# Subtracting the second part of x on VectorE from PSUM, and a state update with 48 columns per head

## The chip, the cores and the metric

The kernel runs on one NeuronCore of a Trainium2 chip. The metric is the device time of one execution in microseconds (us). Engines are named as the profile names them: PE is TensorE's matmul, PEld its weight load, DVE VectorE, ACT ScalarE, POOL GpSimd, SP SyncE (which only issues transfers here).

## The reference, cut to what matters

A linear recurrence with a complex decay per channel runs over 768 tokens for 4 batches and 8 heads of width 48. Its output, 3072 tokens of 384 values, goes through a gated feed-forward layer.

```python
for t in range(S):                                   # S = 768
    S_re, S_im = ar * S_re - ai * S_im, ar * S_im + ai * S_re
    S_re = S_re + outer(k[t], v[t])                  # 48 x 48 per head
    y[t] = q[t] @ S_re
x = y.reshape(3072, 384)
out = ((x @ w_a) * (x @ w_b)) @ w_out                # 384 -> 1536 -> 384
```

## The kernel before, in words

**Units.** The work is cut into 12 units: two batch pairs, each with 6 chunks of 128 tokens. A unit is 2 batches x 128 tokens, so 256 rows of x. For each unit there are four stages.

1. `prep(u)`, nearly all on DVE with some ACT: normalises the decay, forms its running products over the chunk, and multiplies them into q and divides them out of k. It is a Python generator that is advanced a little at a time. `stack(u)` then copies the result by DMA into `stk`, where each head has its 96 rows (48 real, 48 imaginary).
2. `attn(u)`, on PE with short DVE and ACT steps: for each batch i of the two, `scores` (k against q for 4 heads, then a causal mask multiplied in by DVE at L367), `transposes` (k into token rows, copied by ACT at L379), `outputs` (masked scores times v, plus the carried state times q, into the PSUM tile `xp`; ACT copies it at L408 into `xh`, rounded to fp32r), `residual` and `state`.
3. `gemm1(f)`: 18 matmuls for each of 12 blocks f of 128 hidden columns, in fp32r, with x and the weights each split into a rounded part and a remainder: xh·wh, xl·wh, xh·wl. ACT copies one half of the result (L475), DVE multiplies the other half in (L476), ACT rounds it (L477), DVE subtracts to get the remainder (L478).
4. `gemm2(f)`: 6 matmuls into the output, issued three blocks later (LAG = 3).

**The two steps that the change touches.** `residual` forms `xl` = x − `xh`. A matmul with minus the identity as weights (L412) adds −`xh` onto the 384 columns of `xp` still in PSUM, and an ACT copy (L415) takes the remainder out as fp32r. `state` multiplies the transposed k of a head (`kt`, 128 tokens x 96 rows, the weights) by v (the moving operand, 128 tokens x some columns) into a PSUM tile `pm`; DVE then adds it to the carried state `u` (L430), or ACT copies it for the first chunk (L432). In v's packed layout each pair of heads has 128 columns: 0 to 47 are the even head's, 48 to 79 zeros, 80 to 127 the odd head's. The kernel before streams 96 columns per head, 0 to 95 for the even head and 32 to 127 for the odd one, of which `kv` then picks 48. Four heads make a call; each fp32 matmul shows in the profile as two weight loads and two matmul records. `residual` runs 24 times, twice in each unit; `state` runs 40 times, four times in every unit that isn't the last chunk.

**The order.** Unit w's 12 blocks run in a loop. Between `gemm1(f)` and `gemm2` and after it there are slots, from f = 6 on (f = 5 for the first), in which the pieces of `attn(w+1)` are issued two at a time, `residual(0)` after `scores(1,0)` and `residual(1)` after `state(1,0)`. In between, `prep` of a later unit is advanced on DVE by a fixed estimated amount per block. Instructions of attention and of the feed-forward layer are given a higher priority than prep's, so on DVE they stand between prep's instructions. Every engine works its own list strictly in the order in which it was written, so an instruction that waits holds up all behind it. `pm` has two buffers (scores, transposes and state share them), `xp` one, the gemm1 tile `ab` three. PSUM tiles `pm` come free for the next transposes only when DVE has multiplied the mask in.

Of the kernel before, what the change touches and what calls it, by code (L numbers as in the profile page):

```python
# [14 lines left out]
ALU = mybir.AluOpType  # L15
PSUM = bass.MemoryType.PSUM

B, H, S, D = 4, 8, 768, 48
# [24 lines left out]
KS = 2 * D  # L43
# [14 lines left out]
def view(ap, offset, dims):  # L58
    return bass.AP(tensor=ap.tensor, offset=ap.offset + offset, ap=[list(ap.ap[0])] + dims)
# [7 lines left out]
def tile_kernel(ctx: ExitStack, tc: tile.TileContext, a_d, qk_d, v_d, w_d, qn_d, kn_d, vn_d, an_d, out_d):  # L67
    nc = tc.nc
    vec, act, pe, sync = nc.vector, nc.scalar, nc.tensor, nc.sync
# [43 lines left out]
    nident = const.tile([128, 128], F32, name="nident")  # L113
# [4 lines left out]
    def r(ap):  # L118
        return ap.bitcast(F32R)
# [76 lines left out]
    def rescaled(c):  # L196
        return c % 2 == 1 and c + 1 < NCH
# [152 lines left out]
    def attn(u, xh, xl):  # L350

        c = u % NCH
        last = c + 1 == NCH
        ams, kts, xps = {}, {}, {}

        def cols(i):
            return slice(i * C, (i + 1) * C), slice(TOK + i * C, TOK + (i + 1) * C)

        def scores(i, hg):
            qs, ks = cols(i)  # L360
            sp = ps_m.tile([128, 4, 128], F32, name="pm")
            for h4 in range(4):
                h = hg * 4 + h4
                pe.matmul(out=sp[:, h4], lhsT=stk[:, h, ks], rhs=stk[:, h, qs], start=True, stop=True)  # L364
            am = kvp.tile([128, 512], F32, name="am", bufs=2).rearrange("p (h t) -> p h t", h=4)
            with tc.high_priority(offset=ATTN_FIRST):
                vec.tensor_tensor(out=am, in0=sp, in1=mask[:].unsqueeze(1).broadcast_to([128, 4, 128]),  # L367
                                  op=ALU.mult)
            ams[i, hg] = am

        def transposes(i, hg):
            qs, ks = cols(i)
            tp = ps_m.tile([128, 512], F32, name="pm")
            for h4 in range(4):
                pe.transpose(out=tp[:, h4 * KS:(h4 + 1) * KS], in_=stk[0:KS, hg * 4 + h4, ks],
                             identity=ident[0:KS, 0:KS])
            kt = kvp.tile([128, 4, KS], F32, name="kt", bufs=2)
            with tc.high_priority(offset=ATTN_FIRST):
                act.copy(out=kt.rearrange("p h k -> p (h k)"), in_=tp[:, 0:4 * KS])  # L379
            kts[i, hg] = kt  # L380

        def outputs(i, half):
            qs, ks = cols(i)
            v_t = v_tiles[u, i]
            if half == 0:
                xps[i] = ps_x.tile([128, NJ, C], F32, name="xp")
            xp = xps[i]
            work = []
            for qd in range(4):
                lst = []  # L390
                for ti, pieces in quads[qd]:
                    mm = []
                    for h, off in pieces:
                        mm.append((v_t[:, off:off + 32], ams[i, h // 4][:, h % 4, :]))
                        if c > 0:
                            mm.append((us[i][:, off:off + 32], stk[:, h, qs]))
                    for n, (l, rr) in enumerate(mm):
                        lst.append((ti, l, rr, not lst, n == len(mm) - 1))
                work.append(lst)
            ns = len(work[0])  # L400
            for n in range(half * ns // 2, (half + 1) * ns // 2):
                for qd in range(4):
                    ti, l, rr, st, sp_ = work[qd][n]
                    pe.matmul(out=xp[qd * 32:(qd + 1) * 32, ti], lhsT=l, rhs=rr, start=st, stop=sp_,  # L404
                              tile_position=(0, qd * 32), skip_group_check=True)
            if half == 1:
                with tc.high_priority(offset=ATTN_FIRST):
                    act.copy(out=r(xh[:, :, qs]), in_=xp)  # L408

        def residual(i, _):  # L410
            qs, ks = cols(i)
            pe.matmul(out=xps[i], lhsT=r(nident), rhs=r(xh[:, :, qs]), start=False, stop=True,  # L412
                      skip_group_check=True)
            with tc.high_priority(offset=ATTN_FIRST):
                act.copy(out=r(xl[:, :, qs]), in_=xps[i])  # L415

        def state(i, hg):
            ut, v_t = us[i], v_tiles[u, i]
            kp = ps_m.tile([128, 512], F32, name="pm")
            for h4 in range(4):  # L420
                h = hg * 4 + h4
                o = (h // 2) * 128 + (h % 2) * 32
                pe.matmul(out=kp[0:KS, h4 * 96:(h4 + 1) * 96], lhsT=kts[i, hg][:, h4, :],
                          rhs=v_t[:, o:o + 96], start=True, stop=True)
            uv = view(ut[0:KS], hg * 256, [[128, 2], [80, 2], [1, 48]])
            kv = view(kp[0:KS], 0, [[192, 2], [144, 2], [1, 48]])
            sv = view(stk[0:KS], hg * 4 * RUN + 2 * TOK + i, [[2 * RUN, 2], [RUN, 2], [0, 48]])
            with tc.high_priority(offset=ATTN_FIRST):
                if c > 0:
                    vec.tensor_tensor(out=uv, in0=kv, in1=uv, op=ALU.add)  # L430
                else:
                    act.copy(out=uv, in_=kv)  # L432
                if rescaled(c):
                    vec.tensor_tensor(out=uv, in0=uv, in1=sv, op=ALU.mult)

        order = [(scores, 0, 0), (scores, 0, 1), (transposes, 0, 0), (transposes, 0, 1),
                 (outputs, 0, 0), (outputs, 0, 1), (scores, 1, 0), (residual, 0, 0), (state, 0, 0), (scores, 1, 1),
                 (state, 0, 1), (transposes, 1, 0), (transposes, 1, 1), (outputs, 1, 0),
                 (outputs, 1, 1), (state, 1, 0), (residual, 1, 0), (state, 1, 1)]
        if u == 0:  # L440
            order = [(scores, 0, 0), (scores, 0, 1), (outputs, 0, 0), (outputs, 0, 1), (scores, 1, 0), (scores, 1, 1),
                     (residual, 0, 0), (outputs, 1, 0), (outputs, 1, 1), (transposes, 0, 0), (transposes, 0, 1),
                     (residual, 1, 0), (state, 0, 0), (state, 0, 1), (transposes, 1, 0), (transposes, 1, 1),
                     (state, 1, 0), (state, 1, 1)]
        for fn, i, g in order:
            if not (last and fn in (transposes, state)):
                fn(i, g)
                yield
# [292 lines left out]
```

## Time and profile before

| what | value |
|---|---|
| three timed runs | 701.16, 704.75, 705.05 us (median 704.75) |
| the profiled execution's own time | 703.08 us |
| its span from first to last instruction | 701.3 us (1.8 us lie around it) |
| mean granted clock of TensorE | 0.981 |
| PE / PEld / DVE / ACT busy | 654.5 / 608.7 / 553.0 / 319.0 us |
| `residual` matmul L412, ACT copy L415 | 24 of each |
| `state` matmul L423 | 320 records (40 calls x 4 heads x 2) |

Matmul records are pipelined: a gemm1 matmul lasts 0.28 us in the trace while the next one starts 0.11 to 0.12 us after it. So the distance between starts, not the duration, is what a matmul costs PE, and PE shows as busy even where it loses a little. On DVE, too, an instruction's record overlaps the next one's by some tens of nanoseconds.

### The profile page before, as it was taken

Reading aid. Unit: us, or ns where it says so; the run is one execution under the profiler, and the core shown is the slowest. Engines: PE = TensorE matmul, PEld = TensorE weight load, DVE = VectorE, ACT = ScalarE, POOL = GpSimd, SP = SyncE. Lnnn points to the kernel's source line nnn. Section 1 sums busy time; section 2 is a strip of 40 time slices with the busy share of each in tenths; the row PEclk is TensorE's granted clock in tenths of the full one; section 3 lists DMA queues with packets and bytes.
Section 4 is the critical chain, followed back from the end, with each engine's and each line's share of the span. In section 5 each row is a group of like instructions: output and inputs, shape, how many; then the busy total and the mean of one; then the engine's idle time right before and its main releaser. Section 6 shows DMA issues by size and latency. Waiting matters only on the chain.

```text
span 701.3 us, 14492 instructions
## 1 busy us (share of the span) xinstructions
PE 654.5 (93%) x5862; PEld 608.7 (87%) x5862; DVE 553.0 (79%) x1387; ACT 319.0 (45%) x642; POOL 5.6 (1%) x11
## 2 busy tenths in 40 slices
PE   3657899999999999999999999999999999999997
PEld 1224788899898999999999998999999999999996
DVE  6999899898988989989799898999989963232221
ACT  6347666634635446255453554635543332232221
POOL 3000000000000000000000000000000000000000
PEclk9985999999999999999999999999999999999999
DMA  8963300511404206034051250511510510400000
GB/s 317 402 254 91 121 0 2 181 55 46 136 31 141 80 16 197 23 100 122 29 145 59 89 145 2 166 68 47 131 59 2 134 55 7 115 23 2 22 2 28
DMA packets 30233, 63.95 MB, mean 91 GB/s; under 512 B 3664, under 2 KB 7248, under 8 KB 30160
## 3 DMA queue, kind: packets, MB, share of 16 engines
q1 hardware_dynamic: 26704, 58.23, 26.4%
q10 hardware_dynamic: 3456, 4.72, 1.9%
q8 instruction: 48, 0.79, 0.5%
q14 instruction: 25, 0.20, 0.1%
HBM read 39.32 MB, written 4.72 MB: 63 GB/s over the span
## 4 chain that ended last, share of the span: by engine, by line
DVE 55%; PE 31%; ACT 6%; DMA 5%; issue 2%; SPq 0%; DVEq 0%; ACTq 0%
PE ab L467 13%; PE o L485 8%; DVE pr L226 6%; DVE qk L294 5%; DVE a_t L274 5%; DVE z L232 4%; DVE h_t L476 4%; DVE hl L478 4%; PE xp L404 3%; DMA w<-in_dram 3%; PE pm L364 3%; DVE z L279 3%; DVE pb L253 2%; DVE am L367 2%; DVE b_t L259 2%
## 5 line engine op out<-in xcount | busy, mean ns | idle before, releaser
L467 PE MATMUL ab<-xh,w 128*128 128x256 f32 x1728 | 332.5, 282 | 0.0
L467 PEld LDWEIGHTS ab<-xh,w 128*128 128x128 f32 x1728 | 275.6, 189 | 1.9 <-issue 1.0
L467 PE MATMUL ab<-xl,w 128*128 128x256 f32 x864 | 242.2, 280 | 0.0
L467 PEld LDWEIGHTS ab<-xl,w 128*128 128x128 f32 x864 | 162.6, 188 | 0.0
L485 PE MATMUL o<-w,hh 128*128 128x384 f32 x576 | 151.8, 344 | 0.0
L476 DVE TENSOR_TENSOR h_t<-ab,h_t 128x256 f32<-128x256 f32 x144 | 60.3, 419 | 71.3 <-ACT h_t L475 71.3
L475 ACT COPY h_t<-ab 128x256 f32<-128x256 f32 x144 | 53.0, 368 | 133.4 <-PE ab L467 132.3
L477 ACT CAST hh<-h_t 128x256 fp32r<-128x256 f32 x144 | 58.1, 404 | 107.9 <-DVE h_t L476 107.5
L485 PEld LDWEIGHTS o<-w,hh 128*128 128x128 f32 x576 | 96.5, 188 | 3.5 <-issue 3.4
L485 PE MATMUL o<-w,hl 128*128 128x384 f32 x288 | 97.8, 340 | 0.0
L478 DVE TENSOR_TENSOR hl<-h_t,hh 128x256 fp32r<-128x256 f32 x144 | 60.4, 419 | 18.0 <-ACT hh L477 17.8
L226 DVE TENSOR_TENSOR pr<-z 128x192 f32<-128x192 f32 (+1 forms) x195 | 65.2, 341 | 6.0 <-ACT z L212 1.2
L364 PE MATMUL pm<-stk 128*128 128x128 f32 x384 | 55.7, 283 | 4.9 <-DMA stk<-qk 4.3
L364 PEld LDWEIGHTS pm<-stk 128*128 128x128 f32 x384 | 50.2, 195 | 9.0 <-issue 6.4
L146 PE MATMUL ab<-o_sb,ident 128*128 128x384 f32 x42 | 30.6, 830 | 27.3 <-DVE o_sb L137 27.3
L485 PEld LDWEIGHTS o<-w,hl 128*128 128x128 f32 x288 | 54.1, 188 | 0.6 <-issue 0.4
L232 DVE TENSOR_TENSOR z<-pr 128x96 f32<-128x96 f32 (+1 forms) x195 | 47.2, 248 | 3.7
L404 PE MATMUL xp<-am,v_t 128*32 128x128 f32 x768 | 42.2, 277 | 3.8 <-DVE am L367 3.6
L274 DVE TENSOR_TENSOR a_t<-z,b_t 128x768 f32<-128x768 f32 x48 | 45.3, 950 | 0.0
L146 PEld LDWEIGHTS ab<-o_sb,ident 128*128 128x128 f32 x42 | 10.7, 296 | 37.3 <-DVE o_sb L137 27.3
L294 DVE TENSOR_TENSOR qk<-qk,z 128x1536 f32<-128x1536 f32 (+1 forms) x26 | 42.3, 1627 | 0.2
L367 DVE TENSOR_TENSOR am<-pm,mask 128x512 f32<-128x512 f32 x48 | 32.8, 684 | 6.8 <-PE pm L364 6.7
(100 smaller groups left out, 756.5 us busy)
## 6 DMA issues: line engine op xcount, KB each, us to landing
w<-in_dram SPq DMA_DIRECT2D x36, 384.0 KB, 7.9
qk<-in_dram SPq DMA_DIRECT2D x12, 768.0 KB, 4.8
stk<-qk SPq DMA_DIRECT2D x48, 192.0 KB, 3.3
a_t<-in_dram SPq DMA_DIRECT2D x11, 768.0 KB, 4.4
v_t<-in_dram SPq DMA_DIRECT2D x24, 256.0 KB, 2.7
stk<-qk SPq DMA_DIRECT2D x24, 192.8 KB, 3.3
out_dram<-o_sb ACTq DMA_DIRECT2D x24, 192.0 KB, 2.0
stk<-qk SPq DMA_DIRECT2D x16, 128.0 KB, 3.1
```

What stands on the lines that cost most here:

```text
L226: vec.tensor_tensor(out=pr[:, :, :, o:o + n], in0=view(zz, W + at_(i) + 2 * o, [[W, 2], [-W, 2], [2, n]]), in1=tok(slice(1, 3), i - 1, o, ...
L232: vec.tensor_tensor(out=tok(slice(1, 3), i, o, n), in0=pr[:, :, 0, o:o + n], in1=pr[:, :, 1, o:o + n], op=ALU.add)
L274: vec.tensor_tensor(out=pz[:, s].rearrange("p (j b e) -> p j b e", j=SUB // 2, e=2), in0=zb[:, 1 + s], in1=view(bb, (1 + k - s) * NB, [[0, ...
L294: vec.tensor_tensor(out=qk4[:, :, k, x0:x1], in0=qk4[:, :, 1, x0:x1], in1=z[:, k].rearrange("p (j t) -> p j t", j=NJ).unsqueeze(2).broadca ...
L364: pe.matmul(out=sp[:, h4], lhsT=stk[:, h, ks], rhs=stk[:, h, qs], start=True, stop=True)
L404: pe.matmul(out=xp[qd * 32:(qd + 1) * 32, ti], lhsT=l, rhs=rr, start=st, stop=sp_, tile_position=(0, qd * 32), skip_group_check=True)
L467: pe.matmul(out=ab[:, m * TOK:(m + 1) * TOK], lhsT=r(w_ab(f, part, m * NJ + i)), rhs=r(xt[:, i, :]), start=n == 0, stop=n == 8)
L475: act.copy(out=h_t, in_=ab[:, 0:TOK])
L476: vec.tensor_tensor(out=h_t, in0=ab[:, TOK:2 * TOK], in1=h_t, op=ALU.mult)
L477: act.copy(out=r(hh), in_=h_t)
L478: vec.tensor_tensor(out=r(hl), in0=h_t, in1=hh, op=ALU.subtract)
L485: pe.matmul(out=os_[tt][:, 0:DM], lhsT=r(ht[:, ts]), rhs=r(w_t[f, 2][:, part, :]), start=(f == 0 and n == 0), stop=(f == NF - 1 and n == 2))
```

## The change

`residual` no longer uses PE or ACT: DVE subtracts `xh` from the PSUM tile `xp` and writes `xl`. `state` streams only the 48 columns that a head owns, so the four results lie side by side in 192 columns and the picking view `kv` changes with them. Nothing else is changed: the buffers, the slots and the priorities stay.

```diff
         def residual(i, _):
             qs, ks = cols(i)
-            pe.matmul(out=xps[i], lhsT=r(nident), rhs=r(xh[:, :, qs]), start=False, stop=True,
-                      skip_group_check=True)
             with tc.high_priority(offset=ATTN_FIRST):
-                act.copy(out=r(xl[:, :, qs]), in_=xps[i])
+                vec.tensor_tensor(out=r(xl[:, :, qs]), in0=xps[i], in1=xh[:, :, qs], op=ALU.subtract)
 
         def state(i, hg):
             ut, v_t = us[i], v_tiles[u, i]
             kp = ps_m.tile([128, 512], F32, name="pm")
             for h4 in range(4):
                 h = hg * 4 + h4
-                o = (h // 2) * 128 + (h % 2) * 32
-                pe.matmul(out=kp[0:KS, h4 * 96:(h4 + 1) * 96], lhsT=kts[i, hg][:, h4, :],
-                          rhs=v_t[:, o:o + 96], start=True, stop=True)
+                o = (h // 2) * 128 + (h % 2) * 80
+                pe.matmul(out=kp[0:KS, h4 * D:(h4 + 1) * D], lhsT=kts[i, hg][:, h4, :],
+                          rhs=v_t[:, o:o + D], start=True, stop=True)
             uv = view(ut[0:KS], hg * 256, [[128, 2], [80, 2], [1, 48]])
-            kv = view(kp[0:KS], 0, [[192, 2], [144, 2], [1, 48]])
+            kv = view(kp[0:KS], 0, [[2 * D, 2], [D, 2], [1, D]])
```

## The prediction, made before the changed kernel ran

> **What bounds the kernel now.** I read the shares first, then the chain that ended last, because shares alone would name PE.
>
> ```profile
> PE 654.5 (93%) x5862; PEld 608.7 (87%) x5862; DVE 553.0 (79%) x1387; ACT 319.0 (45%) x642; POOL 5.6 (1%) x11
> ```
> ```profile
> DVE 55%; PE 31%; ACT 6%; DMA 5%; issue 2%; SPq 0%; DVEq 0%; ACTq 0%
> ```
>
> PE is busy for 93% of the span, yet DVE holds 55% of the chain. DVE's 79% is an average over two stages, which the table by stretches separates (columns: length, PE, PEld, DVE, ACT busy).
>
> ```profile
> 428.00:473.00 45.00, 44.76 (x454) 43.45 (x455) 41.51 (x102) 22.49 (x44) 0.00 (x0) 1.00 0.30 92
> 558.00:605.00 47.00, 47.00 (x474) 45.85 (x473) 20.70 (x40) 16.22 (x36) 0.00 (x0) 1.00 0.19 57
> ```
>
> While prep runs, DVE is busy 41.5 of 45 us; when prep has ended, 20.7 of 47. What this costs PE is seen in the times at which three successive units start, by their first gemm1 matmul (PE's rows in order of time; units 8, 9 and 10, counted from 0):
>
> ```profile
> 506.42 0.28 PE L467 MATMUL ab<-xh,w 128*128 128x256 f32 x1
> ...
> 557.98 0.28 PE L467 MATMUL ab<-xh,w 128*128 128x256 f32 x1
> ...
> 608.30 0.28 PE L467 MATMUL ab<-xh,w 128*128 128x256 f32 x1
> ```
>
> Units 8 and 9 give PE the same work. Unit 8, with most of a prep beside it, takes 51.56 us, unit 9 50.32. So DVE costs about 1.2 us a unit, and the waits from 250 to 520 us say where:
>
> ```profile
> PEld pm L375 <- DVE am L367: 4.4, 7, 1.6
> ```
> ```profile
> DVE a_t L288 <- ACT a_t L282: 7.5, 7, 1.6
> DVE a_t L303 <- ACT a_t L290: 3.2, 4, 1.9
> ...
> DVE h_t L476 <- ACT h_t L475: 0.3, 1, 0.3
> ```
>
> Transposes wait for a `pm` buffer until DVE has masked the scores. DVE itself waits almost only for ACT's part of prep, and for the feed-forward layer 0.3 us in 270: it is behind PE. The chain shows the end of that state:
>
> ```profile
> 542.81 0.34 DVE hl L478
> 543.14 0.61 DVE am L367
> 543.75 0.05 issue
> 543.80 0.55 PE pm L375 x4
> ```
>
> Up to 543.75 us the chain is mostly DVE, from there on PE alone. So a microsecond added to DVE before 543 should arrive at the end, one taken from PE counts in full only behind it.
>
> **Part 1, the subtraction. What it takes from PE.**
>
> ```profile
> 553.10 0.18 PE xp L412
> ```
> ```profile
> L415 ACT CAST xl<-xp 128x384 fp32r<-128x384 f32 x24 | 11.5, 479 | 12.8 <-PE xp L412 12.6
> ```
>
> The first row is of the chain: an L412 holds PE for 0.18 us, its weight load lying beside the matmul ahead of it. So PE loses 24 x 0.18 = 4.3 us of work. On the PE part of the chain behind 543.75 us lie five of them: the one at 553.10 (second of `attn(9)`) and two each of `attn(10)` and `attn(11)`: **-0.9 us**. The others leave PE earlier at a `pm` wait that DVE ends: nothing, unless DVE is quicker than I think. ACT loses 24 x 0.479 = 11.5 us; at 45% busy, and with no L415 on the chain pieces that I followed, I count that as nothing. If ACT did hold the chain, its 6% share would bound the gain.
>
> **What it adds to DVE.** No 128x384 tensor_tensor stands in the trace, but its neighbours do:
>
> ```profile
> L478 DVE TENSOR_TENSOR hl<-h_t,hh 128x256 fp32r<-128x256 f32 x144 | 60.4, 419 | 18.0 <-ACT hh L477 17.8
> L476 DVE TENSOR_TENSOR h_t<-ab,h_t 128x256 f32<-128x256 f32 x144 | 60.3, 419 | 71.3 <-ACT h_t L475 71.3
> ...
> L137 DVE SCALAR_TENSOR_TENSOR o_sb<-w,o_sb 128x384 uint32<-128x384 uint32 x36 | 19.6, 550 | 0.1
> ```
>
> 384 elements take 550 ns. From PSUM (L476) and from SBUF (L478) 256 elements take the same 419 ns, so the PSUM operand adds nothing. [...]
>
> What the queue loses is the distance between starts. The chain's pieces above give 0.34 for 256 elements (542.81) and 0.61 for 512 (543.14), so about 0.47 for 384. Between two dependent prep instructions it is less, since part of it fills the gap between them:
>
> ```profile
> 416.42 0.36 DVE L226 TENSOR_TENSOR pr<-z 128x192 f32<-128x192 f32 x1
> 416.69 0.42 DVE L478 TENSOR_TENSOR hl<-h_t,hh 128x256 fp32r<-128x256 f32 x1
> 417.03 0.25 DVE L232 TENSOR_TENSOR z<-pr 128x96 f32<-128x96 f32 x1
> 417.31 0.36 DVE L226 TENSOR_TENSOR pr<-z 128x192 f32<-128x192 f32 x1
> 417.71 0.26 DVE L232 TENSOR_TENSOR z<-pr 128x96 f32<-128x96 f32 x1
> 418.00 0.36 DVE L226 TENSOR_TENSOR pr<-z 128x192 f32<-128x192 f32 x1
> ```
>
> A pr-z pair takes 0.89 us with an hl in it (416.42 to 417.31) and 0.69 without (to 418.00), so an instruction that costs 0.34 alone costs 0.20 there. For 384 elements that makes 0.33 to 0.47; I take 0.40, as both kinds of place occur. Fifteen subtractions lie before 543 us in the stage where DVE holds the chain (two each of `attn(2)` to `attn(8)`, one of `attn(9)`): **+6.0 us** (5.0 to 7.1). Those of `attn(0)` and `attn(1)` lie where weight conversion, DMA and PE hold much of the chain: between 0 and 4 x 0.47 = 1.9; I take **+0.7**. The rest fall where DVE is half idle: nothing. If one falls into a wait for ACT (10.7 us in the 270 above), it is free there.
>
> **The wait it adds.** The subtraction waits for ACT's `xh` (L408), and everything behind it on DVE with it: prep, h_t, hl, the masks.
>
> ```profile
> 536.04 0.48 ACT L408 CAST xh<-xp 128x384 fp32r<-128x384 f32 x1 [0.59 <-PE xp L404]
> ```
>
> Since DVE runs behind PE before 543, I take no wait; its bounds are nothing and a whole L408 copy, 0.48 us, each time. Readers of `xl` and the next writer of `xp` come several microseconds of PE work later.
>
> **Part 2, 48 columns.** Halving the moving columns helps only if streaming sets the pace of these matmuls. PE's rows around one call, and the load behind it:
>
> ```profile
> 502.60 0.84 PE L423 MATMUL pm<-v_t,kt 128*96 128x96 f32 x8
> 503.23 0.36 PE L467 MATMUL ab<-xh,w 128*128 128x256 f32 x1
> 503.43 0.28 PE L467 MATMUL ab<-xl,w 128*128 128x256 f32 x1
> ```
> ```profile
> 503.20 0.19 PEld L467 LDWEIGHTS ab<-xh,w 128*128 128x128 f32 x1
> ```
>
> Eight records run from 502.60 to where the last starts, about when the next load does (503.20): 0.60 / 7 = 85 ns each. [...] The first gemm1 matmul behind the call shows what a load then costs: it lasts 0.36 instead of 0.28 us, because its 128-column load began only at 503.20. Loads by columns:
>
> ```profile
> L423 PEld LDWEIGHTS pm<-v_t,kt 128*96 128x96 f32 x320 | 32.2, 164 | 2.1 <-issue 1.4 <-ACT hh L477 0.2 <-DVE z L232 0.2
> L404 PEld LDWEIGHTS xp<-am,v_t 128*32 128x32 f32 x768 | 24.0, 109 | 11.2 <-DVE am L367 5.7 <-issue 2.4 <-ACT xl L415 0.2
> ...
> L375 PEld LDWEIGHTS pm<-ident,stk 96*128 96x128 f32 x160 | 16.2, 143 | 6.5 <-DVE am L367 5.3 <-ACT kt L379 0.2 <-issue 0.2
> ```
>
> From 32 to 96 columns a load grows by 55 ns, 0.86 ns a column; 96 columns are 83 ns, the 85 of the pace. The weights, `kt`, keep their 96 columns. So I take **0** for part 2. Against it speaks that transposes load 128 columns in 143 ns, so not every load goes at that rate. The other bound is that streaming sets the 85 ns: then each record falls to about 43 and PE loses 320 x 42 ns = 13.4 us.
>
> [...]
>
> **The sum.** +6.0 + 0.7 - 0.9 = +5.8 us. The profiled execution took 703.1, so 708.9, and I forecast **709**. The median of the runs shown is 1.7 higher; the bounds and that give 705 to 714 for this case alone. About 1%, 7 us, is what can be told from no change here.
>
> **Rivals.**
>
> *DVE has room after all* (22%). For it: DVE is idle 3.5 of 45 us, and its list is written anew, so subtractions could fall into its waits for ACT. Then PE's 4.3 us are what is left: 698.8. Against it: with room on DVE the chain would not have run 55% there, nor would the masks come late in unit after unit.
>
> *Streaming sets the pace of state* (9%), and PE, so relieved, sets the end: 703.1 - 4.3 - 13.4 = 685.4. For it: a matmul that streams fewer columns keeps the array for less time. Against it: the late load above. If streaming set the pace and DVE still held the chain, only the 4 x 8 records of `attn(10)` in unit 9 would count, 32 x 42 ns = 1.3 us, which stays inside the forecast's range. [...]
>
> *DVE waits for `xh` at the head of its list* (12%). Twenty subtractions before 558 us wait 0.48 each: 9.6 more, 718.5. It decides once the mask and h_t work on DVE is less behind PE than the copy takes; DVE's rows show 0.3 us of waiting for gemm1, which speaks against it.
>
> *The edit does nothing to the work* is excluded for part 1; for part 2 it is my forecast, though PE's records must show 48 columns.
>
> The forecast itself has 52%, and 5% is left for a cause that I don't see. The range 696 to 715 takes the forecast's own and most of the first rival, and leaves out the second and the third. Against the median of 704.75, over 1% is below 697.7 or above 711.8: faster 18% (the second rival and some of the first), slower 30% (the third and the forecast's upper end), within 1% 52%.
>
> **What would show it.** 24 DVE subtractions of about 550 ns and no L412; state records still 85 ns apart, their matmuls shorter; DVE busy about 43 of 45 us in mid-kernel, with longer waits of L375 for the mask; units 9 and 10 0.35 us shorter. State records at 45 ns apart, or DVE waits named after ACT's `xh`, would prove me wrong.

## The result and the profile after

The median after is 708.65 us (707.15 to 710.16, six runs) against 704.64 before: ratio 1.0064, 95% interval [1.0047, 1.0082]. The kernel is 0.6% slower, about 4 us. The profiled execution after, 710.16, is the slowest of its six, that before, 703.08, lies 1.6 under its median, so the traces show 7.1 us between their spans (701.3 and 708.4). The forecast of 709 was right as a number. Its place was wrong: the loss is made in unit 0, and the middle of the kernel, where the sum put +6, did not become slower.

The page of the kernel after, engine shares and the chain by engine:

```profile
PE 658.3 (93%) x5838; PEld 608.8 (86%) x5838; DVE 565.0 (80%) x1411; ACT 309.6 (44%) x618; POOL 5.6 (1%) x11
...
PE 48%; DVE 37%; ACT 5%; DMA 5%; issue 2%; SPq 1%; DVEq 0%; ACTq 0%
```

DVE has 24 instructions and 12 us more, yet its share of the chain fell from 55% to 37%. That alone speaks against "DVE held the chain and now holds it more". The groups of the two edited lines (subtraction, state) and PE's rows around one state call, all of after; lines behind L413 carry numbers two lower than before:

```profile
L413 DVE TENSOR_TENSOR xl<-xp,xh 128x384 fp32r<-128x384 f32 x24 | 13.2, 550 | 3.8 <-ACT xh L408 3.8
L421 PE MATMUL pm<-v_t,kt 128*96 128x48 f32 x320 | 32.9, 246 | 0.1
```
```profile
457.89 0.80 PE L421 MATMUL pm<-v_t,kt 128*96 128x48 f32 x8
458.51 0.36 PE L465 MATMUL ab<-xh,w 128*128 128x256 f32 x1
```

The subtraction takes 550 ns from PSUM, as its SBUF neighbour did, and waited 3.8 us for `xh` in the whole kernel. A call of eight state records with 48 moving columns leaves PE to gemm1 after 458.51 − 457.89 = 0.62 us; with 96 columns it was 503.23 − 502.60 = 0.63.

Where the time went is seen from the start of the feed-forward of unit 0 and of unit 1 (PE's rows in order of time; before, then after):

```profile
80.86 0.36 PE L467 MATMUL ab<-xh,w 128*128 128x256 f32 x1
...
149.97 0.36 PE L467 MATMUL ab<-xh,w 128*128 128x256 f32 x1
```
```profile
79.88 0.60 PE L465 MATMUL ab<-xh,w 128*128 128x256 f32 x3
...
156.88 0.60 PE L465 MATMUL ab<-xh,w 128*128 128x256 f32 x3
```

Unit 0 takes 77.0 us instead of 69.1. From the start of unit 1 to the end it is 708.4 − 156.9 = 551.5 after and 701.3 − 150.0 = 551.3 before. So all of it is made before 157 us. Behind that point units 2 to 4 and 9 lose 3.1 us, units 5 to 8 gain 4.1, unit 11 loses 1.5.

In unit 0 the two chains differ at one place, the end of `prep(1)` (before, then after; start, length, what; L294 is prep's last multiply into q and k):

```profile
125.17 1.67 DVE qk L294
126.86 3.42 DMA stk<-qk
130.32 0.49 PE pm L364 x2
```
```profile
129.28 1.67 DVE qk L294
130.95 0.34 DVE h_t L474
131.29 0.51 DVE qk L294
131.79 1.07 issue
132.87 0.43 DVE hl L476
133.30 0.27 SPq L331
...
135.68 4.23 DMA stk<-qk
139.95 0.81 PE pm L364 x2
```

Before, prep's last multiply starts at 125.1 us and `stk` reaches the scores of `attn(1)` from 130.3 on. After, it starts at 131.2, the first piece of `stk` comes at 136.40 and the last at 139.95. What PE does meanwhile (after, PE's rows; in brackets the idle time ahead and what ended it):

```profile
134.14 0.34 PE L483 MATMUL o<-w,hl 128*128 128x384 f32 x1
136.40 1.01 PE L364 MATMUL pm<-stk 128*128 128x128 f32 x4 [1.92 <-DMA stk<-qk]
138.79 0.46 PE L364 MATMUL pm<-stk 128*128 128x128 f32 x2 [1.38 <-DMA stk<-qk]
139.95 1.49 PE L364 MATMUL pm<-stk 128*128 128x128 f32 x4 [0.70 <-DMA stk<-qk]
```

PE has used up all of unit 0's gemm2 by 134.5 and can do nothing but wait. Before, gemm2 matmuls still stood between the scores, the last of them at 139.1 us. A second thing happens here, in the table by stretches (length, PE, PEld, DVE, ACT, POOL busy, then the granted clock; before, then after):

```profile
140.00:144.00 4.00, 3.49 (x58) 3.11 (x47) 3.86 (x10) 2.15 (x4) 0.00 (x0) 1.00 0.33 117
```
```profile
136.00:140.00 4.00, 1.48 (x7) 0.94 (x7) 3.18 (x9) 2.84 (x4) 0.00 (x0) 0.93 0.88 268
140.00:144.00 4.00, 3.91 (x31) 2.75 (x32) 2.97 (x9) 2.43 (x4) 0.00 (x0) 0.50 0.49 133
144.00:148.00 4.00, 3.43 (x25) 2.96 (x28) 3.22 (x8) 1.88 (x3) 0.00 (x0) 0.71 0.63 201
```

Just when PE has work again its clock is halved, for 0.6 + 4.0 + 2.3 = 6.9 us by the three shares (a stretch at 0.71 is half-speed for 0.58 of it); stretches cut at its edges place it from 139.46 to 146.29 us, 6.8 us.

Over the whole kernel the waits turned around (60 to 710 us; total, times, longest; before, then after):

```profile
PE pm L364 <- DMA stk<-qk: 4.3, 4, 1.7
...
PE pm L375 <- DVE am L367: 3.4, 7, 1.3
```
```profile
PE pm L364 <- DMA stk<-qk: 9.3, 9, 1.9
...
PE pm L375 <- DVE am L367: 0.6, 2, 0.4
```

The transposes' wait for the mask, which I had expected to grow, nearly vanished; the wait for `stk` doubled, and 4.0 of its 9.3 us lie in unit 0 (0.7 of the 4.3 before).

### The profile page after: what moved, and what is told of

Its sections match the earlier page's. It is cut to its first block, busy times and chain, and to the rows that moved or that the text cites. A ratio compares the mean times of both kernels' runs of the same rounds, so it can differ in the third digit from the quotient of the medians.

```text
span 708.4 us, 14429 instructions
## 1 busy us (share of the span) xinstructions
PE 658.3 (93%) x5838; PEld 608.8 (86%) x5838; DVE 565.0 (80%) x1411; ACT 309.6 (44%) x618; POOL 5.6 (1%) x11
## 4 chain that ended last, share of the span: by engine, by line
PE 48%; DVE 37%; ACT 5%; DMA 5%; issue 2%; SPq 1%; DVEq 0%; ACTq 0%
PE ab L465 21%; PE o L483 10%; PE xp L404 6%; PE pm L364 4%; DVE qk L294 4%; DVE a_t L274 4%; DVE pr L226 4%; PE pm L421 3%; DMA stk<-qk 3%; DVE hl L476 3%; DVE h_t L474 3%; DVE z L232 2%; PE pm L375 2%; DVE z L279 2%; DVE pb L253 2%
## 5 line engine op out<-in xcount | busy, mean ns | idle before, releaser
L364 PE MATMUL pm<-stk 128*128 128x128 f32 x384 | 60.7, 291 | 10.1 <-DMA stk<-qk 9.3
L364 PEld LDWEIGHTS pm<-stk 128*128 128x128 f32 x384 | 52.3, 199 | 16.4 <-issue 9.9
L404 PE MATMUL xp<-am,v_t 128*32 128x128 f32 x768 | 45.2, 283 | 2.7 <-DVE am L367 2.7
L294 DVE TENSOR_TENSOR qk<-qk,z 128x1536 f32<-128x1536 f32 (+1 forms) x26 | 42.3, 1628 | 0.1
```

Of the source, the lines that this page charges most:

```text
L294: vec.tensor_tensor(out=qk4[:, :, k, x0:x1], in0=qk4[:, :, 1, x0:x1], in1=z[:, k].rearrange("p (j t) -> p j t", j=NJ).unsqueeze(2).broadca ...
```

## The experiments

Each ratio is to the kernel before, which ran again beside each group: its medians were 703.13 (e1 to e4), 702.93 (e5 to e8) and 703.16 (e9, e10), so a ratio is not the quotient of the medians in this table. "prep(1)" is when DVE starts prep(1)'s last L294, "unit 1" when its first gemm1 matmul starts, "between" the time from one to the other, "half clock" how long TensorE ran at half rate from 120 to 160 us, "rest" the span minus "unit 1". These five come from the one profiled execution of each. That execution lies within 1 us of its kernel's median but for before (1.6 below), e10 (1.7 below), e8 (1.3 above), after (1.5 above), e9 (2.0 above) and e4 (4.4 above).

| kernel | median us | ratio, interval | prep(1) | unit 1 | between | half clock | rest |
|---|---|---|---|---|---|---|---|
| before | 704.64 | | 125.1 | 150.0 | 24.9 | 0 | 551.3 |
| after | 708.65 | 1.0064 [1.0047, 1.0082] | 131.2 | 156.9 | 25.7 | 6.8 | 551.5 |
| e1 part 1 alone | 704.72 | 1.0020 [1.0006, 1.0033] | 127.5 | 151.0 | 23.4 | 0 | 551.8 |
| e2 part 2 alone | 702.77 | 0.9999 [0.9986, 1.0011] | 126.6 | 150.0 | 23.5 | 0 | 550.9 |
| e3 from unit 2 on | 702.10 | 0.9981 [0.9966, 0.9995] | 126.6 | 150.1 | 23.5 | 0 | 550.2 |
| e4 units 0, 1 only | 709.15 | 1.0073 [1.0054, 1.0092] | 131.3 | 158.5 | 27.2 | 10.2 | 553.3 |
| e5 e3, subtracted twice | 711.55 | 1.0115 [1.0094, 1.0136] | 125.9 | 149.5 | 23.5 | 0 | 559.6 |
| e6 48 weight columns | 705.01 | 1.0027 [1.0008, 1.0046] | 128.7 | 155.0 | 26.3 | 13.7 | 548.6 |
| e7 from unit 1 on | 703.85 | 1.0013 [0.9997, 1.0029] | 126.0 | 149.3 | 23.4 | 0 | 552.6 |
| e8 no priority in units 0, 1 | 705.98 | 1.0030 [1.0011, 1.0048] | 130.7 | 154.1 | 23.4 | 0 | 551.5 |
| e9 scores repeated | 707.31 | 1.0050 [1.0031, 1.0069] | 130.3 | 155.4 | 25.0 | 3.4 | 552.2 |
| e10 before, prep(1) later | 709.91 | 1.0090 [1.0065, 1.0115] | 128.8 | 152.6 | 23.8 | 3.4 | 553.8 |

The columns "between" and "half clock" hold what the forecast had no term for. In the six edited kernels that stay at full rate (e1, e2, e3, e5, e7, e8) unit 1 starts 23.4 to 23.5 us behind prep(1)'s last multiply, whether that stands at 126 or at 131 us: unit 1 follows prep(1) one for one. Before, it is 24.9, so prep(1) had about 1.4 us of slack there. Of the 6.9 us that unit 1 starts later in after, prep(1) gives 6.1 − 1.4 = 4.7, and 25.7 − 23.5 = 2.2 come with the half clock.

**The two parts apart.** e1 has part 1's lines and before's `state`; e2 has part 2's and before's `residual`.

> Part 1 alone: the subtraction on VectorE, state with 96 columns as before. Three theories. DVE theory (the prediction's): each of some 15 subtractions in units 1 to 8 costs 0.33 to 0.47 us on the chain: about 704.6 + 5.8 = 710. Unit-0 theory: the loss is made in unit 0, where the changed profile has prep(1) end 6 us later and unit 0 take 77.0 instead of 69.1 us; the other units end up about even; part 2 is worth nothing, so 708 to 709, as the whole change. List-order theory: any edit rewrites the order of the engines' lists and moves unit 0 by some microseconds, whatever its work; then the time can lie anywhere from 701 to 712.

> Part 2 alone: 48 columns, the remainder by matmul and ScalarE copy as before. Weight loads set the pace (prediction, and also the unit-0 theory): state records stay 85 ns apart, time as before, 704.6 within 1 us. Streaming sets the pace: 42 ns apart, up to 13 us faster. List-order theory: pace 85 ns, but unit 0 and with it the time moves by 2 us or more either way.

Part 2 alone changes nothing (1.000). Part 1 alone costs 0.2%, far less than the 0.6% of both. No price per instruction gives that: 24 equal subtractions cost 1.4 us in one kernel and 4 in the other. What differs is the order in which the planner (the program that orders each engine's instructions) wrote the lists (DVE's rows from prep(0) to prep(1) stand in another order), and with it prep(1): 127.5 us in e1, 131.2 in after.

**Where the subtractions cost.** e3 keeps the matmul and the copy in `attn(0)` and `attn(1)`, e7 in `attn(0)` alone, e4 in all others; all have 48 columns.

```diff
         def residual(i, _):
             qs, ks = cols(i)
+            if u >= 2:          # e7: u >= 1, e4: u < 2
+                with tc.high_priority(offset=ATTN_FIRST):
+                    vec.tensor_tensor(out=r(xl[:, :, qs]), in0=xps[i], in1=xh[:, :, qs], op=ALU.subtract)
+                return
             pe.matmul(out=xps[i], lhsT=r(nident), rhs=r(xh[:, :, qs]), start=False, stop=True,
                       skip_group_check=True)
```

> The whole change, but the attention of units 0 and 1 (which runs before and in unit 0 of the loop) forms the remainder as before; 20 of 24 subtractions stay on VectorE. DVE theory: 704.6 + 6.0 - 0.9 = 709.7. Unit-0 theory: unit 0 goes back to about 69 us, and what is left is the gain of up to 20 x 0.18 = 3.6 us on TensorE less what VectorE costs in the middle: 701 to 705. List-order theory: unit 0 may stay long all the same.

> The counterpart: only the four subtractions of the attention of units 0 and 1 are on VectorE, the other 20 remainders as before, 48 columns throughout. DVE theory: 704.6 + 0.7 = 705.3. Unit-0 theory: nearly the whole loss, unit 0 of the loop 75 to 78 us, the time 709 to 712, as the other units lose TensorE's gain. List-order theory: open.

> The whole change, but only the attention of unit 0 forms the remainder as before. Its two subtractions stand ahead of the end of prep(1) on VectorE; those of the attention of unit 1 stand behind it. If the loss in unit 0 of the loop comes through prep(1), this run is like that from unit 2 on: 701.5 to 703, unit 0 at 70 us. If it comes through the attention of unit 1, it stays near 708.

The four subtractions of `attn(0)` and `attn(1)` cost 0.73%, the whole loss. The other twenty cost nothing on balance: e3 is 0.2% faster than before, slightly better than both kernels. With only `attn(0)` put back, e7 lies within its uncertainty of no change, and its prep(1) and unit 1 are as early as e3's. So the loss at unit 1 takes the first two, those that DVE does while it forms prep(1). Those of `attn(1)` are not shown to be free: e7 is 0.3% slower than e3, the intervals do not meet, and its rest is 2.3 us longer.

**Is there room on DVE?** e5 is e3 with each of its twenty subtractions written twice.

```diff
                 with tc.high_priority(offset=ATTN_FIRST):
                     vec.tensor_tensor(out=r(xl[:, :, qs]), in0=xps[i], in1=xh[:, :, qs], op=ALU.subtract)
+                    vec.tensor_tensor(out=r(xl[:, :, qs]), in0=xps[i], in1=xh[:, :, qs], op=ALU.subtract)
```

> As the run with the subtraction from unit 2 on (702.1 us), with each of those 20 subtractions done twice on VectorE, the second time over the first one's result. DVE theory: the second 15 in units 1 to 8 cost 0.33 to 0.47 us each, so 5 to 7 us more, 707 to 709. Room theory: VectorE has room in the middle of the kernel, its long chain there is only the order of its list: 702 to 703.5.

The second set costs 711.55 − 702.10 = 9.4 us (by the ratios too, 1.3%), 0.47 for each, while the first set cost nothing. PE's waits from 170 to 560 us, of e3 and of e5:

```profile
PE pm L364 <- DMA stk<-qk: 5.0, 6, 1.5
PE pm L375 <- DVE am L367: 0.2, 1, 0.2
```
```profile
PE pm L364 <- DMA stk<-qk: 8.5, 9, 1.6
```

DVE's room shows as how late prep may end. The last multiply of prep(9) and the first scores of `attn(9)`, which read `stk` (before, then after):

```profile
485.12 1.75 DVE L294 TENSOR_TENSOR qk<-qk,z 128x1536 f32<-128x1536 f32 x1
...
527.54 1.95 PE L364 MATMUL pm<-stk 128*128 128x128 f32 x16
```
```profile
514.46 1.75 DVE L294 TENSOR_TENSOR qk<-qk,z 128x1536 f32<-128x1536 f32 x1
...
533.32 1.95 PE L364 MATMUL pm<-stk 128*128 128x128 f32 x16
```

Before, 42 us lie between the two starts, after and in e3 19. The multiply and the transfer alone take 5.2 us, as in unit 0 before (125.1 to 130.3), so 5.2 is no lead at all. The first set used up part of the lead. In e5 the same multiply starts at 528.3 us and the scores at 533.5: prep(2) to prep(10) all stand at 4.8 to 5.3, and with the lead gone a further subtraction costs its whole distance of 0.47.

The lead is built up unit by unit. Before, prep(1) to prep(3) have none (5.2 each), prep(4) has 9.5, prep(9) 42.4; in after and e3 prep(1) to prep(5) have none.

**What sets the pace of state.** e6 is the change with weights of 48 columns too. It leaves out the imaginary half of the state update.

```diff
-                pe.matmul(out=kp[0:KS, h4 * D:(h4 + 1) * D], lhsT=kts[i, hg][:, h4, :],
+                pe.matmul(out=kp[0:D, h4 * D:(h4 + 1) * D], lhsT=kts[i, hg][:, h4, 0:D],
                           rhs=v_t[:, o:o + D], start=True, stop=True)
```

> The whole change, and state loads only 48 of the 96 columns of k as weights, so that only the real half of the carried state is updated and the imaginary half stays zero. If weight loads set the pace of state, its records come 45 ns apart instead of 85 and TensorE has 320 x 40 ns = 12.8 us less to do; where TensorE holds the units, the time falls from 708.7 by 8 to 13 us, where VectorE holds them, by 2 or less. If it was neither streaming nor loads but the issue of instructions, the pace stays at 85 ns.

Starts within a call are 45 ns apart (median) instead of 85 with the same 48 moving columns; from the first to the next gemm1 it is 405.58 − 405.09 = 0.49 us, against 0.62:

```profile
405.09 0.56 PE L421 MATMUL pm<-v_t,kt 128*48 128x48 f32 x8
405.58 0.39 PE L465 MATMUL ab<-xh,w 128*128 128x256 f32 x1
```

Halving the moving columns changed nothing, halving the weight columns did: here the loads set the pace. But PE gained next to nothing of the 12.8 us expected: the call starts 0.27 us behind the start of the matmul ahead of it (404.82 to 405.09) instead of 0.18 (457.71 to 457.89 in after), and the first gemm1 matmul behind it lasts 0.39 us instead of 0.36. From the gemm2 matmul ahead of the call to the second gemm1 matmul behind it, it is 404.82 to 405.80, 0.98 us, against 457.71 to 458.71, 1.00, in after. So the 2.9 us by which its rest is shorter than after's are not explained by the pace. Its unit 1 is late for the reason below: prep(1) stands at 128.7, and the half clock lasts 13.7 us.

**Order in the list.** e8 is the whole change, with the subtractions of `attn(0)` and `attn(1)` at ordinary priority.

```diff
-            with tc.high_priority(offset=ATTN_FIRST):
+            with tc.high_priority(offset=ATTN_FIRST if u >= 2 else 0):
```

> The whole change with the same work, but the four subtractions of the attention of units 0 and 1 without the raised priority, so that VectorE's list in unit 0 is written in another order (the first subtraction behind a mask and a prep step, the second behind a dozen prep steps). Work theory: the subtractions themselves and their wait cost the 6 us in unit 0; prep(1) ends as late, 708 to 710. List-order theory: what costs is that weight conversion and gemm1 steps were written ahead of prep(1)'s last steps; with another order unit 0 comes to 70 to 72 us and the time to 702 to 704.

Half of the loss goes (1.003). prep(1) is only 0.5 us earlier than in after, yet unit 1 starts 2.8 us earlier. The other 2.3 are the difference in "between", 25.7 against 23.4: e8 has no half clock here. Its gemm1 of unit 0 starts 5.4 us later (85.3), so PE still has gemm2 matmuls until 139.5 us, where after had its last at 134.1. Unit 0 is in another order altogether: it shows that order moves this stage by microseconds, not which order is best.

**The clock and the wait.** e9 repeats the first four score matmuls of `attn(1)`, to fill the hole (24 added records); e10 is the kernel before, with five more DVE multiplies in prep(1) whose results are written over.

```diff
                 h = hg * 4 + h4
-                pe.matmul(out=sp[:, h4], lhsT=stk[:, h, ks], rhs=stk[:, h, qs], start=True, stop=True)
+                for _ in range(4 if (u, i, hg) == (1, 0, 0) else 1):
+                    pe.matmul(out=sp[:, h4], lhsT=stk[:, h, ks], rhs=stk[:, h, qs], start=True, stop=True)
```
```diff
+        if u == 1:
+            for _ in range(5):
+                vec.tensor_tensor(out=a_t[:, 1], in0=a_t[:, 0], in1=a_t[:, 0], op=ALU.mult)
```

> The whole change; in unit 0 the four score matmuls of attn(1), on stk's first two heads, are issued four times each instead of once (same result, 24 more fp32 record pairs of 128 columns, about 2.7 us of TensorE work at 112 ns each). They stand where TensorE waited for stk's transfer at 136 to 140 us in the changed kernel, so they fill part of the hole behind 136. If the half clock of 139.5 to 146.3 us is what costs unit 0 a part of its 77.0 us, and it comes from TensorE having been idle: the granted clock stays 1.0 between 136 and 148, unit 0 comes down to 73 to 75 and the time to 705 to 707. If the half clock is only a mark beside the wait: the clock falls as before or does not, but unit 0 keeps its 77 us or grows by the added work, and the time is 708.5 to 711.5.

> The kernel before with nothing of the change; prep(1) does five more multiplies of 128x768 on DVE (0.87 us each by their rows, 4.35 us in all; their results are written over). Theory now held (unit 0's loss is prep(1) ending late, whatever made it late): prep(1) ends near 129.5 us instead of 125.1, stk's transfer comes later by that much, TensorE waits for it in unit 0, and the time is 4.4 us above the kernel before without a fall of the clock (707 to 709), up to 7 above with one (710). Rival (the loss belongs to the subtractions themselves, in attn(0) and attn(1), through PSUM or xh): prep(1) late by 4.4 us is absorbed as it is in the middle of the kernel, where prep ended 14 us later at no cost: 703 to 705.

e9 is inconclusive. The clock fell all the same, earlier and for half as long; the added matmuls, too, begin only when `stk` comes, at 135.56 us after 1.94 us of waiting (stretches of e9):

```profile
132.00:136.00 4.00, 2.06 (x12) 1.74 (x11) 3.64 (x9) 2.87 (x5) 0.00 (x0) 0.95 0.58 149
136.00:140.00 4.00, 4.00 (x25) 4.00 (x25) 3.37 (x10) 2.82 (x5) 0.00 (x0) 0.62 0.84 236
```

Its interval overlaps that of after. A price of the half clock does not come out of the table: above 23.5, "between" is longer by 0.3 (e10) and 1.5 (e9, with added matmuls) at 3.4 us of it, by 2.2 at 6.8 (after), 3.7 at 10.2 (e4) and 2.8 at 13.7 (e6), one execution of each.

e10 shows the mechanism without the change. With the old `residual` and 96 columns, prep(1) comes 3.7 us later, unit 1 starts 2.6 later, and the kernel is 0.9% slower than before. The rival, that the loss belongs to the subtractions themselves (703 to 705), is refuted for unit 0. Its chain runs over the same place, and PE's rows show the hole there:

```profile
128.92 1.68 DVE qk L294
130.61 3.21 DMA stk<-qk
133.87 0.78 PE pm L367 x2
```
```profile
132.78 0.91 PE L146 MATMUL pm<-o_sb,ident 128*128 128x384 f32 x2 [1.77 <-DVE o_sb L137]
133.87 0.78 PE L367 MATMUL pm<-stk 128*128 128x128 f32 x2 [0.18 <-DMA stk<-qk]
```

By contrast prep(10) starts its last L294 at 543.1 us in e2 instead of 528.6, at no cost: it still ends 35 us ahead of its scores. A late prep is dear where the scores wait for it, as in unit 0, and free where it has a lead. e10 has two blurs. The multiplies also delayed the weight conversions on DVE (PE waits 1.8 us for `o_sb`), but two matmuls later PE would have stood before the scores all the same, which begin when `stk` comes. And its rest is 2.5 us longer than before's, spread over units 1 to 5, which I can't place: unit 0 accounts for 2.6 us of the 5.1 between the two traces.

## Why the prediction was right in number and wrong in place

The 709 is luck: a loss of 6 us in the middle did not come, and one of about that size came in unit 0, where the sum had 0.7.

- **Part 2 at 0: right,** for the reason given. Pace 85 ns with 96 and 48 moving columns, 45 with 48 weight columns, e2 at 1.000. The rival "streaming sets the pace of state" (685.4) is refuted. A state record lasts 248 ns (median) in both traces, so it did not get shorter. Of the loads in the trace before, all 4320 of state, gemm1, gemm2, scores and transposes, 96 or 128 columns each, begin no earlier than the matmul before them starts; of the 1408 32-column loads of `outputs` (L404) 1184 begin earlier, by up to 0.15 us.
- **The subtraction's duration, 550 ns and nothing extra for PSUM: right,** and so was its distance in a queue without room, 0.33 to 0.47: e5 measured 0.47.
- **"+6.0 us" for fifteen subtractions in the middle: wrong.** Together with PE's relief the middle lost nothing: units 1 to 10 take 504.5 us before, 503.1 after, 503.3 in e3 (504.1 in e2, which has no subtraction, so 1 us either way may be the list). The step that failed is "a microsecond added to DVE before 543 should arrive at the end". I took DVE's 55% of the chain, 41.5 busy us of 45 and the waits for the mask as proof that DVE was behind. Those waits fell from 3.4 to 0.6 us with more work on DVE, and DVE's own waits of h_t for ACT rose from 1.5 to 10.3 us (60 to 545 us): an engine that is behind does not wait for the feed-forward layer like that. Whether DVE is behind shows in another number, the lead with which prep ends ahead of the scores that read it. It was behind in units 0 to 2 before (prep(1) to prep(3) without a lead) and far ahead later, 42 us for prep(9). The rival "DVE has room after all" (698.8) was right from there on; but the middle gained 1.4 us of the 4.3 that it counted. Units 2 to 4 lose 2.3 us, where prep has no lead in after; whether the subtractions did that is not shown, as e2 too loses 1.2 in units 2 and 3 and gains 1.3 in unit 4.
- **"+0.7" for `attn(0)` and `attn(1)`, bounds 0 to 1.9: mis-sized.** Measured +4 to +5 by medians (e4 1.0073) and 6.9 us at the start of unit 1 in the traces. I priced only the DVE time of four instructions. prep(1) has no lead. Between prep(0)'s last L294 and the first whole one of prep(1), after has 69.0 us instead of 63.4: DVE is busy 2.6 us longer (two more h_t, two more hl, two subtractions, one more o_sb) and idle 2.9 longer. In e1 the same two subtractions stand there, but with one more h_t and hl and 0.3 us more idle time it takes 65.7. From 60 to 131 us two of these waits read, in after:

```profile
DVE h_t L474 <- ACT h_t L473: 1.6, 2, 0.9
...
DVE xl L413 <- ACT xh L408: 0.9, 1, 0.9
```

  Before, h_t's waits for ACT stay below 0.5 us there. Then come a later transfer, a PE with nothing left to do, and the half clock, in place of the 0.7: 4.7 us by prep(1) and 2.2 with the half clock.
- **"−0.9" behind 543.75 us: not seen.** Unit 10 is 0.2 us shorter, unit 9 is 0.8 longer, where prep now runs on to 604 us. Unit 11 is 1.5 longer in after and not in e3 or e4; that stays open.
- **"DVE waits for `xh`" (718.5): small.** 3.8 us in total and not 9.6; only the 0.9 in unit 0 lies where it counts.
- **The range of the sum:** the bounds of its terms (5.0 to 7.1, 0 to 1.9, −0.9) give 707.2 to 711.2, or 712.9 with the 1.7 of the median, and not 705 to 714; 705 needs a gain that no term held.
- **Not tried:** the change with e1's list order, which would say whether the four subtractions must cost anything. Why the planner writes another list with 48 columns is open too.

## What to carry to other kernels

When an engine prepares data ahead, measure its lead (end of the preparation to first use) unit by unit before pricing an addition: with a lead it costs nothing until the lead is used up (here e3's twenty subtractions, ratio 0.998; e5's further twenty, 0.47 us each), and here the first units have none (three before, five after). An engine's share of the chain and the waits behind a shared in-order list don't show that it is behind, since a planner that rewrites the list can move those waits (here 3.4 us of waiting for the mask became 0.6). In a start-up stage bound the cost of an edit by what a late hand-over leaves the next engine to do, not by the added instructions' time; and try the edit with the first units left as they were (here 702.1 instead of 708.65).

## What the runs showed of the hardware

The granted clock of TensorE fell in mid-run without a long pause of PE: in after its longest single wait in the 7 us ahead of the fall was 1.92 us. The half-rate stretches near unit 1 last 3.4 us (e9, e10), 6.8 (after), 10.2 (e4) and 13.7 (e6): one, two, three and four times the shortest. In a stretch of that length, half of after's 6.83 us, just ahead of the fall PE was busy 1.44 us in after (136.05 to 139.46), 1.47 in e9, 1.46 in e10 and 1.43 in e4. Behind 1.85 (132.63 to 136.05 of after) and 1.78 (138.67 to 142.09 of e3) it stayed at 1.0; behind 1.53 in e4 (133.00 to 136.42) it stayed once too. What makes the clock fall, and for how long, is not shown by these runs.
